# Experts: token numbers kept with an item's rows and stored with y, rows of x loaded two items ahead, routing of tiles 24 to 31 ahead of the queue of side work

## The chip, the cores and the metric

The kernel runs on one core of one Trainium2 chip. The metric is the device time of one launch in microseconds, given as the median of several runs. Beside these stands one profiled execution, from which the trace comes; its time is given apart, since it is not one of the runs of the median.

## The reference

Three layers follow one another, all in float32. Attention has 8 x 8 heads of 576 queries with 64 columns, whose keys and values are averaged over groups of 8 first; its output is read as 4608 tokens x 512 columns. Then each token goes to one of 8 experts, chosen by the cosine of the token with the expert's embedding, and then comes a plain feed-forward layer with h * cos(h) between its two products.

```python
k_p, v_p = mean over groups of 8 of k, v             # 72 keys per head
x = softmax(q @ k_p.T / 8) @ v_p                     # 4608 tokens x 512
logits = (x/|x|) @ (emb/|emb|).T / tau               # 8 experts
expert_idx, gate_w = argmax(logits), softmax(logits)[expert_idx]
for e in range(8):
    h = np.maximum(x[expert_idx == e] @ w1[e], 0.0)  # 512 -> 1024
    out[expert_idx == e] = gate_w * (h @ w2[e])      # 1024 -> 512
h = out @ w_in                                       # 512 -> 2048
return (h * np.cos(h)) @ w_out                       # 2048 -> 512
```

## The kernel before

Every large product is made of three: each operand is split into a rounded high part and the rest (`hi` and `lo`, `xhi` and `xlo`, `ha` and so on), and hi x hi, hi x lo and lo x hi are added up in PSUM. A split is a copy on ScalarE (`w_hi`, line 127, for weights) followed by a subtraction on VectorE or GpSimd (`w_lo`, line 130). The program is written out by hand: the order of the calls is the order of each engine's queue.

**Attention and routing.** `phase_a` goes through 36 tiles of 128 tokens in steps n = -3 to 37 (`step`); a step holds attention for one tile, with products, evacuations and softmax parts of several tiles staggered. After 9, 18, 24, 28, 32, 34 and 36 tiles (`CHUNKS`), `route` gives two lists of short operations for the tiles of the chunk: the gate, the expert and the place `DEST` of each token in its expert's region of the DRAM buffer `xv`. Those lists are put into the queue `side`, from which `pump` takes a few operations at given places of each step. When 32 tiles (`EARLY`) are through, `pick` follows in the same queue: it chooses the expert with the most tokens so far, writes the table `tab0` for the first item, and issues the fetch of its first weights. `scatter(n)` then has GpSimd send a tile's rows to `xv` by an indirect DMA. A row has 514 columns: 512 of x, the gate, and the token's number. After the last step come the scatters left over, the load of the first item's rows, the routing of the last tiles, and the splits of the first weights.

**Expert items.** An item is up to 512 rows of one expert (wide: 8 of them in this run, counting item 0) or 256 (narrow: 5). It has 16 steps k: 8 products of the first layer, `gemm1` (matmuls `ph`, then ReLU and split into `ha`, `hb`), and 8 half products of the second, `gemm2` (matmuls `py`, result in `ys`). Within an item stand, at steps that the tables `FIRST`, `WIDE` and `NARROW` give: the weights' `fetch` and splits for this and the next item, the multiplication of the next item's rows by their gates (`gate`, line 747, ScalarE), and the transposes of these rows (`t_x`: matmuls `ptx` at line 752, then the copy to `xhi` and the subtraction to `xlo`). The rows of the next item come by `x_load` (line 740) at the start of an item, into four buffers `xr`; the item's result goes out at its end by `y_store` into the DRAM buffer `yv`, ordered by item. All loads and stores but the indirect ones are issued by SyncE, in program order; an issue that waits for a buffer holds back those behind it.

In item 0, twelve operations at a time (`LATE`), VectorE works out the tables `tab` of all items between the first-layer products (`tables`); when they are done, zero rows are stored behind each expert's rows, and the loads for item 1 follow (`mid0`). In items 1 to 4 GpSimd sends each tile's token numbers, 4 bytes a token, to their places in the DRAM buffer `pv` (`pos_scatter`, line 797, 36 in all): the feed-forward layer needs them to write its output rows back in token order. `conv_part` converts the feed-forward weights (given as float64) to float32 on VectorE, in 7 short operations for each of 32 pieces, from item 0 on.

**Feed-forward.** In the first narrow item `prepare` loads and splits the first weights and the first 512 columns of input (`f_load`, `f_split`, `x2_load`, `x2_split`). Then nine groups of 512 tokens by 16 slices f follow: `ff1` (matmuls at line 937), `act`, `ff2` (line 961), and the weights are split during the first group, on ScalarE and GpSimd.

## Time and profile before

| | |
|---|---|
| median of three runs | 1595.54 us (1589.47 to 1596.8) |
| the profiled execution | 1583.44 us, of which its span is 1581.70 |
| mean granted TensorE clock | 0.966 of full speed |
| TensorE busy | 1454.1 us, 92% of the span |
| first product of item 0 | 208.05 us after the span's start |
| first product of item 1, of item 5 | 275.45, 506.19 |
| first product of the first narrow item | 647.60 |
| first product of feed-forward | 774.35 |

The span is the profiled execution from its first instruction to its last; what the execution's time has beyond it lies ahead of and behind the program. The lower rows are times on the trace's own clock, from which the length of each stage is read: attention and routing, item 0, items 1 to 4, the other wide items, the narrow items, and feed-forward to the end.

### The profile page before, as it was taken

Reading aid. Unit: us, or ns where it says so; the run is one execution under the profiler, and the core shown is the slowest. Engines: PE = TensorE matmul, PEld = TensorE weight load, DVE = VectorE, ACT = ScalarE, POOL = GpSimd, SP = SyncE. Lnnn points to the kernel's source line nnn. Section 1 sums busy time; section 2 is a strip of 40 time slices with the busy share of each in tenths; the row PEclk is TensorE's granted clock in tenths of the full one; section 3 lists DMA queues with packets and bytes.
Section 4 is the critical chain, followed back from the end, with each engine's and each line's share of the span. In section 5 each row is a group of like instructions: output and inputs, shape, how many; then the busy total and the mean of one; then the engine's idle time right before and its main releaser. Section 6 shows DMA issues by size and latency. Waiting matters only on the chain.

```text
span 1581.7 us, 20523 instructions
## 1 busy us (share of the span) xinstructions
PE 1454.1 (92%) x7480; PEld 1231.9 (78%) x7480; DVE 933.0 (59%) x1623; ACT 609.6 (39%) x1006; POOL 485.1 (31%) x377
## 2 busy tenths in 40 slices
PE   4999667498999999999899999999999999999996
PEld 4898556376777888899787888888888888888885
DVE  5788764365656652344488656565656565565653
ACT  4898533133333444555533222232323222222321
POOL 4578531436553444353444101020201011010200
PEclk9999878789999999999999999999999999999998
DMA  9865437867998655586531101010100000010000
GB/s 264 229 187 151 161 125 231 134 173 192 179 238 216 215 190 170 200 267 214 175 92 56 52 1 54 1 54 1 54 1 27 27 27 28 1 54 1 27 1 27
DMA packets 91877, 177.77 MB, mean 112 GB/s; under 512 B 16236, under 2 KB 35180, under 8 KB 91764
## 3 DMA queue, kind: packets, MB, share of 16 engines
q1 hardware_dynamic: 84688, 157.38, 36.2%
q0 software_dynamic: 6912, 18.94, 3.3%
q8 instruction: 62, 1.02, 0.3%
q14 instruction: 55, 0.42, 0.1%
q10 hardware_dynamic: 160, 0.02, 0.0%
HBM read 135.87 MB, written 40.43 MB: 111 GB/s over the span
## 4 chain that ended last, share of the span: by engine, by line
PE 39%; issue 5%; DVE 4%; ACT 1%; POOL 1%; DVEq 0%; POOLq 0%; ACTq 0%
PE ph L937 20%; PE po L961 20%; DVE xhi L951 2%; DVE ys L947 1%; DVE ys L949 1%; ACT ys L948 1%; DVE co L946 0%; DVE xhi L950 0%; POOL out_dram L972 0%; POOL ha L923 0%; ACT ha L922 0%; ACT ys L945 0%; DVEq L950 0%; POOLq L971 0%; POOLq L972 0%
## 5 line engine op out<-in xcount | busy, mean ns | idle before, releaser
L130 POOL TENSOR_TENSOR lo<-raw,hi 128x1024 fp32r<-128x1024 f32 x82 | 196.6, 2403 | 305.6 <-ACT hi L127 268.7
L945 ACT ACTIVATE ys<-ph,quarter 128x512 f32<-128x512 f32 x144 | 99.0, 688 | 297.1 <-PE ph L937 296.8
L961 PE MATMUL po<-hi,xhi 128*128 128x512 f32 x576 | 178.9, 390 | 0.2
L948 ACT ACTIVATE ys<-ys 128x512 f32<-128x512 f32 x144 | 91.0, 632 | 227.6 <-DVE ys L947 227.6
L951 DVE TENSOR_TENSOR xhi<-ys,xhi 128x512 fp32r<-128x512 f32 x144 | 159.7, 1109 | 5.1
L961 PE MATMUL po<-fh,xhi 128*128 128x512 f32 x504 | 157.1, 392 | 2.8 <-DVE xhi L951 2.2
L949 DVE TENSOR_TENSOR ys<-ys,ph 128x512 f32<-128x512 f32 x144 | 99.1, 688 | 100.6 <-ACT ys L948 100.6
L946 DVE TENSOR_SCALAR co<-ys 128x512 f32<-128x512 f32 x144 | 63.2, 439 | 155.9 <-ACT ys L945 155.9
L762 PE MATMUL ph<-xhi,hi 128*128 128x512 f32 (+1 forms) x416 | 101.2, 366 | 53.7 <-DVE hb L766 36.0
L777 PE MATMUL py<-ha,hi 128*128 128x256 f32 (+1 forms) x576 | 142.6, 340 | 0.1
L961 PEld LDWEIGHTS po<-hi,xhi 128*128 128x128 f32 x576 | 108.2, 188 | 24.8 <-DVE xhi L951 2.5
L762 PEld LDWEIGHTS ph<-xhi,hi 128*128 128x128 f32 x416 | 71.5, 196 | 69.5 <-DVE hb L766 37.6
L127 ACT ACTIVATE hi<-raw 128x1024 fp32r<-128x1024 f32 x108 | 112.1, 1053 | 6.3 <-DMA raw<-in_moe_w_dram 4.9
L961 PEld LDWEIGHTS po<-fh,xhi 128*128 128x128 f32 x504 | 95.0, 188 | 24.4 <-DVE xhi L951 3.8
L961 PE MATMUL po<-lo,xhi 128*128 128x512 f32 x288 | 112.1, 389 | 0.0
L777 PEld LDWEIGHTS py<-ha,hi 128*128 128x128 f32 x576 | 97.9, 193 | 9.7 <-DVE ha L766 0.3
L923 POOL TENSOR_TENSOR hb<-craw,hb 128x1024 fp32r<-128x1024 f32 x10 | 25.1, 2518 | 260.9 <-ACT hb L922 260.9
L947 DVE TENSOR_TENSOR ys<-ys,co 128x512 f32<-128x512 f32 x144 | 99.7, 692 | 4.9
L961 PE MATMUL po<-fl,xhi 128*128 128x512 f32 x252 | 98.6, 391 | 0.0
L762 PE MATMUL ph<-xlo,hi 128*128 128x512 f32 (+1 forms) x416 | 98.4, 360 | 0.0
L762 PE MATMUL ph<-xhi,lo 128*128 128x512 f32 (+1 forms) x416 | 97.0, 356 | 0.0
L777 PE MATMUL py<-ha,lo 128*128 128x256 f32 (+1 forms) x288 | 96.1, 334 | 0.0
(211 smaller groups left out, 2891.4 us busy)
## 6 DMA issues: line engine op xcount, KB each, us to landing
raw<-in_moe_w_dram SPq DMA_DIRECT2D x116, 512.0 KB, 5.5
xr<-xv SPq DMA_DIRECT2D x46, 257.0 KB, 6.8
kraw<-in_k_dram SPq DMA_DIRECT2D x12, 768.0 KB, 9.0
vraw<-in_v_dram SPq DMA_DIRECT2D x8, 1152.0 KB
craw<-yv SPq DMA_DIRECT2D x9, 1024.0 KB, 5.4
q<-in_q_dram SPq DMA_DIRECT2D x8, 1024.0 KB
craw<-in_moe_w_in_dram SPq DMA_DIRECT2D x16, 512.0 KB
craw<-in_moe_w_out_dram SPq DMA_DIRECT2D x16, 512.0 KB, 4.5
```

What stands on the lines that cost most here:

```text
L127: nc.scalar.activation(HI[c], RAW[c], AF.Copy)
L130: eng.tensor_tensor(LO[c], RAW[c], HI[c].bitcast(F32), ALU.subtract)
L762: nc.tensor.matmul(p[:, 0:w], W[kk][:, f * 128:(f + 1) * 128], x[:, kk, 0:w], start=(c == 0), stop=(c == 3 * KC - 1))
L777: nc.tensor.matmul(p[:, 0:w], W[4 + f // 2][:, o:o + 128], h_at(f, m, w), start=(f == 0 and c == 0), stop=(f == FC1 - 1 and c == 2))
L937: nc.tensor.matmul(p, wf(f, s, 0)[:, kk * 128:(kk + 1) * 128], x2[:, m * KC + kk, :], start=(c == 0), stop=(c == 3 * KC - 1))
L945: nc.scalar.activation(u, p, AF.Identity, scale=1.0 / TWO_PI_EXACT, bias=quarter)
L946: nc.vector.tensor_scalar(nr, u, MAGIC, MAGIC, op0=ALU.add, op1=ALU.subtract)
L947: nc.vector.tensor_tensor(u, u, nr, ALU.subtract)
L948: nc.scalar.activation(u, u, AF.Sin, scale=TWO_PI)
L949: nc.vector.tensor_tensor(u, u, p, ALU.mult)
L951: nc.vector.tensor_tensor(gl, u, gh.bitcast(F32), ALU.subtract)
L961: nc.tensor.matmul(O[g][r], a[:, r * 128:(r + 1) * 128], wf(f, s, 1), start=(f == 0 and c == 0), stop=(f == FC2 - 1 and c == 2))
```

## The change

- *Token numbers.* `pos_scatter`, the places `COLI` and their four table steps go. A row's number, which lies in column 513 of `xr`, is transposed by one more TensorE operation per tile in `t_x`, into a PSUM bank `pp`; after an item's last tile ScalarE copies the item's numbers to `pt`, and `pos_store` sends them to `pv`, which is now ordered as `yv` is, by a plain DMA at the start of the item. For the first item the numbers lie in a row of `ys` until then.
- *Rows of x.* `x_load` for the rows of the item after the next one stands at an item's end, ahead of `y_store`, and no longer at the next item's start. The gates of wide items stand after steps 8, 9, 11 and 13, in place of 4 to 7. The weights' fetches move from ahead of steps 8 and 14 to behind 6 and 13.
- *Routing.* The fifth chunk (tiles 28 to 31) is routed at step 33 directly and no longer through `side`, with `pick` in its middle, and its scatters, the load of the first item's rows and the weights' fetch stand in step 34. The `hi` splits of the first weights stand in the last steps; two of the `lo` splits go to GpSimd; the last tiles' second list and their scatters go into the operations of item 0. Item 0's gates stand on VectorE.
- *Zero rows* are stored as soon as the last places are known, ahead of the tables and not behind them.
- *Conversion* in item 0 begins at step 8, in place of 10.
- *Preparation of feed-forward* in the first narrow item: `x2_load` at step 0, in place of 8; `x2_split` at 6 and 7, in place of 13 and 14; three weights are split there on VectorE, in place of one on GpSimd, and more are loaded.

```diff
-    pv = dram.tile([REG + 128, 1], F32, name="pv")
+    pv = dram.tile([1, NT + 512], F32, name="pv")
...
+    def zero_rows():
+
+        for e in range(E):
+            row = nc.sync.value_load(basei[0:1, e:e + 1], min_val=e * REG, max_val=e * REG + NT)
+            d = nc.sync.dma_start(xv[bass.ds(row, 128), :], zeros)
+            apart("xv_rows", d)
+            SENT.append(d)
...
+            if n == EARLY + 2:
+                for f in early[1]:
+                    f()
...
+            if n == EARLY + 2:
+                for f in early[2]:
+                    f()
+                for i in range(EARLY - 4, EARLY):
+                    scatter(i)
+                x_load(tab0, 0, 4)
+                fetch(tab0, 0, 4, 1)
             for c0, c1 in chunks[:-1]:
-                if n == c1 + 1:
+                if n == c1 + 1 == EARLY + 1:
+                    assert c0 == EARLY - 4 and not side and not todo
+                    f1, f2 = route(c0, c1, sm, lambda: misc("pr"))
+                    early.update({1: f1[-1:] + [f2[1], f2[3]] + pick(sm), 2: [f2[0], f2[2]] + f2[4:]})
+                    for f in f1[:-1]:
+                        f()
+                elif n == c1 + 1:
                     f1, f2 = route(c0, c1, sm, lambda: misc("pr"))
                     side.extend(f1[:-2] + [None, f1[-2]] + ([None] if c1 < RL else []) + [f1[-1]] + f2 + [lambda c0=c0, c1=c1: todo.extend(range(c0, c1))])
-                    if c1 == EARLY:
-                        side.extend(pick(sm))
-            if PN <= n <= N:
+            if n >= PN:
                 while todo and todo[0] < EARLY:
                     scatter(todo.pop(0))
             if n < PN:
                 pump(PU, 1)
             else:
                 pump(PF if n <= N else len(side), 2)
+            if n > N - 1:
+                for c in range(2 * (n - N), 2 * (n - N) + 2):
+                    w_hi(c)
...
+        V.tensor_copy(basei, base)
+        V.ops.append(zero_rows)
...
+        def gate(r, first=False):
+            if first:
+                nc.vector.tensor_scalar(xr[r][:, 0:DM], xr[r][:, 0:DM], xr[r][:, DM:DM + 1], None, op0=ALU.mult)
+            else:
+                nc.scalar.activation(xr[r][:, 0:DM], xr[r][:, 0:DM], AF.Copy, scale=xr[r][:, DM:DM + 1])
+
+        PT_ = {}
+
+        def t_x(r, n, b=0, out=1):
             p = bank(b, "ptx")
             for kk in range(KC):
                 nc.tensor.transpose(p[:, kk * 128:(kk + 1) * 128], xr[r][:, kk * 128:(kk + 1) * 128], ident)
             pv_, s = p.rearrange("p (k n) -> p k n", k=KC), slice(r * 128, (r + 1) * 128)
             nc.scalar.activation(XHI[:, :, s], pv_, AF.Copy)
             nc.vector.tensor_tensor(XLO[:, :, s], pv_, XHI[:, :, s].bitcast(F32), ALU.subtract)
+            if r == 0:
+                PT_[0] = bank(6, "pp")
+            nc.tensor.transpose(PT_[0][0:1, s], xr[r][:, DM + 1:XW], ident)
+            if r == n - 1:
+                nc.scalar.activation(pt[out][:, 0:n * 128], PT_[0][0:1, 0:n * 128], AF.Copy)
...
-        def pos_scatter(n):
-            nc.gpsimd.engine_nop()
-            d = nc.gpsimd.indirect_dma_start(
-                out=pv, out_offset=bass.IndirectOffsetOnAxis(ap=COLI[:, n:n + 1], axis=0),
-                in_=GT[:, n, 1:2], in_offset=None,
-            )
-            apart("pos", d)
-            POSD.append(d)
+        def pos_store(i, w, out=1):
+            col = nc.sync.value_load(tab[i:i + 1, 4:5], min_val=0, max_val=NT)
+            nc.sync.dma_start(pv[:, bass.ds(col, w)], pt[out][:, 0:w])
...
-            w1c, w2c, on_dve, gates, txs = when
+            w1c, w2c, on_dve, gates, txs, (at2, at1) = when
             if i:
-                x_load(tab, i + 1, n)
+                pos_store(i, w)
             for k in range(16):
-                if k == 8:
-                    fetch(tab, i + 1, 5, 1)
-                if k == 14 and i:
-                    fetch(tab, i + 2, 5, 0)
                 if k < 8:
                     gemm1(k, w)
-                    if mid:
-                        mid(k)
                 else:
-                    for r in gates.get(k, ()):
-                        gate(r)
                     gemm2(k // 2 - 4, k % 2, w)
                     for r in txs.get(k, ()):
-                        t_x(r)
-                    if mid:
-                        mid(k)
+                        t_x(r, n)
+                if mid:
+                    mid(k)
                 for c in (w2c if k < 8 else w1c).get(k, ()):
                     w_hi(c)
                     w_lo(c, nc.vector if c in on_dve else nc.gpsimd)
+                if k == at2:
+                    fetch(tab, i + 1, 5, 1)
+                if k == at1:
+                    fetch(tab, i + 2, 5, 0)
                 if conv:
                     conv(k)
-                if k < 8:
-                    for r in gates.get(k, ()):
-                        gate(r)
-            if not i:
-                fetch(tab, 2, 5, 0)
+                for r in gates.get(k, ()):
+                    gate(r)
+            x_load(tab, i + 2, n)
...
-        WIDE = {8 + k: (k,) for k in range(4)}, {k: (4 + k,) for k in range(4)}, (), {4 + k: (k,) for k in range(4)}, {9: (0,), 11: (1,), 13: (2,), 15: (3,)}
...
+        WIDE = {8 + k: (k,) for k in range(4)}, {k: (4 + k,) for k in range(4)}, (), {8: (0,), 9: (1,), 11: (2,), 13: (3,)}, {9: (0,), 11: (1,), 13: (2,), 15: (3,)}, (6, 13)
...
-        while todo and todo[0] < EARLY:
-            scatter(todo.pop(0))
-        x_load(tab0, 0, 4)
-        fetch(tab0, 0, 4, 1)
-        f1, f2 = route(NTILE - CHUNKS[-1], NTILE, const, lambda: bank(6, "pr"))
         while todo:
             scatter(todo.pop(0))
-        for f in f1:
+        f1, f2 = route(NTILE - CHUNKS[-1], NTILE, const, lambda: bank(7, "pr"))
+        for f in f1[:-1]:
             f()
-        for c in range(4):
-            w_hi(c)
-            w_lo(c, nc.vector)
-        for f in f2:
-            f()
-        for i in range(NTILE - CHUNKS[-1], NTILE):
-            scatter(i)
-        zeros = second_part()
-        late = tables(co[0], craw[0][:, 0, :])
+        pt.append(ys[0:1, 3, :])
         for r in range(4):
-            gate(r)
+            gate(r, True)
         for r in range(4):
-            t_x(r, (0, 3, 4, 5)[r])
...
-        def mid0(n):
-            if n < 8:
+            t_x(r, 4, (0, 3, 4, 5)[r], 0)
+            w_lo(r, nc.vector if r < 2 else nc.gpsimd)
+        f1[-1]()
+        second_part()
+        late = f2 + [lambda: [scatter(i) for i in range(NTILE - CHUNKS[-1], NTILE)]] + tables(ys[:, 0, :])
+
+        def mid0(k):
+            if k < 8:
                 for f in late[:LATE]:
                     f()
                 del late[:LATE]
-                if not late and zeros is not None and not once:
+                if not late and not once:
                     once.append(1)
-                    zero_rows(zeros)
+                    pos_store(0, 512, 0)
                     x_load(tab, 1, 4)
                     fetch(tab, 1, 5, 0)
-                    conv_load(0)
-                    conv_load(1)
+                    for j in range(2):
+                        conv_load(j)
 
         once = []
-        item(0, 512, conv_part(0, 10, 16), mid0, FIRST)
+        item(0, 512, conv_part(0, 8, 16), mid0, FIRST)
         assert once
         for i in range(1, NW0):
-            item(i, 512, conv_part(i, 0, 16), lambda k, i=i: pos_scatter((i - 1) * 9 + k) if k < 9 else None, WIDE)
...
         def prepare(k):
             if k == 0:
                 f_load(0)
-            if k == 8:
                 x2_load(0)
-            if k == 10:
-                f_split(0)
-            if k in (13, 14):
-                x2_split(0, k - 13)
+            if k == 5:
+                f_split(0, nc.vector)
+            if k in (6, 7):
+                x2_split(0, k - 6)
+            if k == 7:
+                for f in range(1, 4):
+                    f_load(f)
+            if k in (13, 15):
+                f_split(1 + k // 15, nc.vector)
             if k == 15:
-                for f in range(1, 4):
+                for f in (4, 5):
                     f_load(f)
...
-        f_split(1)
         seq = [(g, f) for g in range(NG) for f in range(FC2)]
         NS = len(seq)
         for n in range(NS + 2):
-            if n + 2 < FC2:
-                f_split(n + 2)
-                if 4 <= n + 4 < FC2:
-                    f_load(n + 4)
+            if n + 3 < FC2:
+                f_split(n + 3)
+                if n + 6 < FC2:
+                    f_load(n + 6)
```

Three places show how this moves instructions. The first is SyncE's queue at the end of an item; L785 and L811 are the store of an item's result, L740 and L234 the loads of rows into `xr`, L815 is the store of token numbers. Before, at the end of item 0 and the start of item 1:

```order
L784 TENSOR_LOAD tab
L784 ISA x2
L785 REGISTER_ALU
L785 DMA yv<-ys 512x1x512
L739 TENSOR_LOAD tab
L739 ISA x2
L740 ISA
L740 DMA xr_102<-xv 128x514
L739 TENSOR_LOAD tab
L739 ISA x2
L740 ISA
L740 DMA xr_103<-xv 128x514
```

and now, from the last of the four row loads on:

```order
L233 TENSOR_LOAD tab
L233 ISA x2
L234 ISA
L234 DMA xr_105<-xv 128x514
L810 TENSOR_LOAD tab
L810 ISA x2
L811 REGISTER_ALU
L811 DMA yv<-ys 512x1x512
L814 TENSOR_LOAD tab
L814 ISA x2
L815 REGISTER_ALU
L815 DMA pv<-pt 1x512
```

All four row loads now stand ahead of the store; the numbers' store of the item that begins follows it.

The second place is ScalarE in the first narrow item, around its last first-layer products; `ha` is the ReLU of a product, L127 the high part of a weight, L747 and L766 the gate, L781 and L807 the result, L754 and L775 the copy of transposed rows, L910 and L916 the split of a feed-forward weight, L926 that of the feed-forward input. Before:

```order
L765 ACTIVATE ha<-ph 128x256 x2
L127 ACTIVATE hi_2525<-raw_114 128x1024
L765 ACTIVATE ha<-ph 128x256
L747 ACTIVATE xr_102<-xr_102 128x512
L765 ACTIVATE ha<-ph 128x256
L747 ACTIVATE xr_103<-xr_103 128x512
L127 ACTIVATE hi_98<-raw_107 128x1024
L781 ACTIVATE ys<-py 128x256
L754 ACTIVATE xhi<-ptx 128x4x128
L127 ACTIVATE hi_99<-raw_108 128x1024
L910 ACTIVATE fh_2634<-ys 128x1024
```

and now:

```order
L791 ACTIVATE ha<-ph 128x256 x2
L916 ACTIVATE fh_2657<-ys 128x1024
L127 ACTIVATE hi_2583<-raw_114 128x1024
L791 ACTIVATE ha<-ph 128x256
L926 ACTIVATE hb<-craw 128x1024
L791 ACTIVATE ha<-ph 128x256
L926 ACTIVATE hb<-craw 128x1024
L766 ACTIVATE xr_102<-xr_102 128x512
L127 ACTIVATE hi_98<-raw_107 128x1024
L807 ACTIVATE ys<-py 128x256
```

The feed-forward weight stood behind the item's first result and now stands ahead of its last two `ha`; the splits of the input, which stood at the item's end, follow these two.

The third place is VectorE where the first expert is chosen, in attention's last steps; L430 to L432 and L448 to L450 belong to a tile's attention output, L383 and L401 are the maximum of the last tiles' scores, L203 to L213 are `pick`. Before:

```order
L430 TENSOR_TENSOR lp<-pav,rd 128x64
L431 TENSOR_TENSOR x<-pav,rd 128x512
L432 TENSOR_REDUCE LG<-lp 128x8
L203 TENSOR_TENSOR pc<-base,ebase 128x8
L204 TENSOR_REDUCE pm<-pc 128x1
L205 TENSOR_SCALAR pt<-pc,pm 128x8
L206 TENSOR_TENSOR pt<-pt,idx_73 128x8
L207 TENSOR_REDUCE pk_2280<-pt 128x1
L208 TENSOR_SCALAR first_e<-idx_73,pk_2280 128x8
L209 TENSOR_SCALAR pk_2280<-pk_2280 128x1
L210 TENSOR_SCALAR tab_93<-pk_2280 128x1
L426 TENSOR_SCALAR rd<-pav 128x8
```

and now, with the same maximum that before stands some way ahead of these rows:

```order
L401 TENSOR_REDUCE mx<-psc 128x8
L185 TENSOR_TENSOR rt_2310<-pr,base 128x32
L187 TENSOR_TENSOR base<-base,pr 128x8
L203 TENSOR_TENSOR pc<-base,ebase 128x8
L204 TENSOR_REDUCE pm<-pc 128x1
L205 TENSOR_SCALAR pt<-pc,pm 128x8
L206 TENSOR_TENSOR pt<-pt,idx_73 128x8
L207 TENSOR_REDUCE pk_2314<-pt 128x1
L208 TENSOR_SCALAR first_e<-idx_73,pk_2314 128x8
L209 TENSOR_SCALAR pk_2314<-pk_2314 128x1
L210 TENSOR_SCALAR tab_92<-pk_2314 128x1
L211 TENSOR_SCALAR tab_92<-pk_2314 128x1
```

The two operations of `route` on which the choice rests (L185, L187) and the choice itself now follow that maximum directly; the rest of `route` comes behind them.

## Rows read from the trace of the kernel before

**Rows 1.** The page, part 1: busy time of TensorE, its share, its matmuls.
```profile
PE 1454.1 (92%) x7480; PEld 1231.9 (78%) x7480; DVE 933.0 (59%) x1623; ACT 609.6 (39%) x1006; POOL 485.1 (31%) x377
```

**Rows 2.** Timeline of TensorE: start, length in us; last, the wait before and who ended it.
```profile
203.65 3.67 PE L752 MATMUL ptx<-ident,xr 128*128 128x128 f32 x16 [9.87 <-ACT xr L747]
208.05 2.05 PE L762 MATMUL ph<-xhi,hi 128*128 128x512 f32 x4 [0.73 <-issue]
227.77 2.07 PE L762 MATMUL ph<-xhi,hi 128*128 128x512 f32 x4 [6.58 <-DVE ha L766]
265.37 1.11 PE L752 MATMUL ptx<-ident,xr 128*128 128x128 f32 x4 [7.30 <-DVE xlo L755]
275.45 1.44 PE L762 MATMUL ph<-xhi,hi 128*128 128x512 f32 x4 [0.74 <-ACT xhi L754]
318.83 1.65 PE L762 MATMUL ph<-xhi,hi 128*128 128x512 f32 x3 [23.77 <-DVE hb L766]
506.19 1.19 PE L762 MATMUL ph<-xhi,hi 128*128 128x512 f32 x4 [0.80 <-ACT xhi L754]
552.68 1.19 PE L762 MATMUL ph<-xhi,hi 128*128 128x512 f32 x4 [0.80 <-ACT xhi L754]
647.60 0.73 PE L762 MATMUL ph<-xhi,hi 128*128 128x256 f32 x4 [2.75 <-ACTq L1023]
774.35 1.16 PE L937 MATMUL ph<-hb,fh 128*128 128x512 f32 x4 [2.75 <-PEq L1046]
787.66 0.51 PE L961 MATMUL po<-fh,xhi 128*128 128x512 f32 x1 [2.19 <-DVE xhi L951]
```

**Rows 3.** The loads of token rows (L740): who waited for them; time to landing.
```profile
  ACT xr L747: 51.2, 6
DMA to landing us min/median/max: 2.6/6.8/26.9
```

**Rows 4.** Timeline of SyncE's queue in the second item.
```profile
289.82 6.60 SPq L740 DMA_DIRECT2D xr<-xv  x4
```

**Rows 5.** DMA from 288 to 318 us: all packets, then the queue of GpSimd's DMAs.
```profile
DMA packets 2330, 4.97 MB, mean 166 GB/s; under 512 B 436, under 2 KB 568, under 8 KB 2330
q0 software_dynamic: 256, 0.00, 2.1%
```

**Rows 6.** DMA from 510 to 525 us, when no token number is scattered.
```profile
DMA packets 1983, 3.61 MB, mean 241 GB/s; under 512 B 144, under 2 KB 573, under 8 KB 1981
```

**Rows 7.** Groups by line, GpSimd: the scatters of token numbers, busy us and mean ns.
```profile
L797 POOL DMA_INDIRECT pv<-GT,COLI x36 | 35.0, 973 | 8.6 <-issue 8.6
```

**Rows 8.** Timeline of TensorE: four transposes of one tile of token rows.
```profile
254.73 0.60 PE L752 MATMUL ptx<-ident,xr 128*128 128x128 f32 x4
```

**Rows 9.** Timeline of VectorE and SyncE's queue at the end of attention.
```profile
176.34 0.76 DVE L383 TENSOR_REDUCE mx<-psc 128x8 f32<-128x576 f32 x1
184.10 0.16 DVE L203 TENSOR_TENSOR pc<-base,ebase 128x8 f32<-128x8 f32 x1
197.62 2.60 SPq L740 DMA_DIRECT2D xr<-xv  x3
```

**Rows 10.** Timeline of GpSimd and VectorE while the first item's weights are split.
```profile
217.41 9.34 POOL L130 TENSOR_TENSOR lo<-raw,hi 128x1024 fp32r<-128x1024 f32 x4 [3.71 <-ACT hi L127]
217.52 2.38 DVE L634 TENSOR_TENSOR co<-co 128x64 f32<-128x64 f32 x1
```

**Rows 11.** Timeline of VectorE where the first conversion of feed-forward weights begins.
```profile
259.65 0.69 DVE L860 TENSOR_SCALAR ca<-craw 128x512 uint32<-128x512 uint32 x1 [17.00 <-DMA craw<-in_moe_w_in_dram]
264.64 0.68 DVE L755 TENSOR_TENSOR xlo<-ptx,xhi 128x512 fp32r<-128x512 f32 x1
```

**Rows 12.** Timeline of SyncE's queue in the first narrow item.
```profile
645.14 0.60 SPq L785 DMA_DIRECT2D yv<-ys  x1
660.88 0.66 SPq L914 DMA_DIRECT2D craw<-yv  x1
```

**Rows 13.** The loads of feed-forward input (L914): time to landing.
```profile
DMA to landing us min/median/max: 5.4/5.4/5.5
```

71 lines of the change are left out of this document (26 added, 45 removed).

## The prediction

> **What bounds the kernel now.** I read the page first: TensorE is busy for 92% of the span [rows 1], so the kernel can lose time only where TensorE waits or has its clock lowered. The second view is TensorE's timeline, of which I kept the matmuls that had waited and the first matmul of some items [rows 2]. The reader is to see that two wide items in a row without a wait are 552.68 - 506.19 = 46.49 us apart, and that the four items from 275.45 to 506.19 take 230.74 us where 4 x 46.49 = 185.96 would do: 44.8 us are lost in items 1 to 4. The longest single wait there is 23.77 us. It names VectorE's `hb`, which waits in turn for ScalarE, and ScalarE stands at the gating of the next item's rows: the third view, the loads of `xr`, gives 51.2 us of such waiting in six places, and a slowest landing of 26.9 us against a fastest of 2.6 [rows 3]. Fourth, the DMA: while that slow load (issued from 289.82 on [rows 4]) is under way, 4.97 MB move at 166 GB/s, and the queue with the 4-byte scatters of token numbers takes only 2.1% itself [rows 5]; four items later, when no number is scattered, much the same mix (a y store, four row loads, a conversion) moves at 241 GB/s [rows 6] and nobody waits. Ahead of item 1 lie a wait of 9.87 us for the first item's rows, and waits of 6.58 and 7.30 us inside item 0 [rows 2].
>
> **The change part by part.** The sum is made against the profiled execution's own 1583.44 us (span 1581.70 and 1.74 around it). That lies 12.1 us under the median of the three runs, 1595.54; I apply the same difference to the median.
>
> *Items 1 to 4.* The 36 scatters on GpSimd, 973 ns each [rows 7], go. The load of rows stands at almost the same place in SyncE's queue as before, but ahead of the y store instead of behind it, and the gate moves from after product 4 to after step 8, so four steps of 46.49 / 16 = 2.9 us, 11.6 us, are added to the time that a load may take. Items 5 to 7, where nothing was scattered, had no wait even with the early gate. I take the whole 44.8 us: -44.8. The other bound is -30, if the second item's load is late once more (below). GpSimd's freed 35 us are worth nothing by themselves, since its splits were waited for nowhere in these items.
>
> *Token numbers through TensorE.* Each tile of rows gets one more transpose, one column wide. No row shows such a column; the nearest is four transposes of full width in 0.60 us [rows 8], so 0.15 each as the upper price and 0 as the lower. There are 8 x 4 + 5 x 2 = 42 tiles; the last one of each of the 13 items falls into the wait for `xhi` that stands ahead of the next item anyway (0.74 to 0.80 us [rows 2]), so 29 x 0.15 = 4.4: +4. ScalarE's copy of the numbers and the 2 KB store are one each per item and lie beside the first products of the next item, which leave both idle; without that cover 13 copies at 0.69 (a step of 512 columns) would cost 9.
>
> *Routing of tiles 28 to 31.* The choice of the first expert now begins behind the maximum at 176.34 (0.76 long), not at 184.10 [rows 9]: 7.0 us earlier, and with it the fetch of the first weights on SyncE. The rows come later than that: their load, at 197.62 now, waits for the last scatters of x, whose four descriptors GpSimd still writes one after the other, and the work that used to lie behind it (the splits of LO, the last tiles' routing) is moved off the path. Attention itself pays for some 20 short VectorE operations put ahead of a tile's own. Between 0 and -7 I take -5 for the start of item 0 at 208.05.
>
> *Inside item 0.* The tables run beside GpSimd's four splits of the second weights (217.41, 9.34 us), and a table step that takes two operands from SBUF stands 2.38 us there [rows 10]; that is the 6.58 us wait. The splits and the tables both stay, the tail of routing (11 short steps) now stands ahead of the tables, so the wait moves one product on and keeps its size. The zero rows leave the middle of the queue, so row, weight and conversion loads are issued earlier; but conversion begins two steps earlier in the program too, and ten of its steps, not seven (7 took 264.64 - 259.65 = 5.0 us [rows 11]), now stand on VectorE ahead of the first `xlo`. What is won on arrival is mostly spent in that line: -2, with bounds of -13.9 (both waits gone) and +5.
>
> *Feed-forward preparation in the first narrow item.* The load of the feed-forward input is now the third DMA of that item, where before it stood behind the second weights and was issued at 660.88 [rows 12]; it lands 5.4 us after issue [rows 13]. ScalarE has its copies of that data, and of the first feed-forward weights, ahead of the `ha` of products 6 and 7. Those fall due about 647.60 + 7 x 1.45 = 657.8 (half of 2.9 a step). The load must wait for the y store of 645.14 to land; with 5.4 for that megabyte too and some 3.5 for the end of the branch and the two DMAs ahead, I estimate its issue at 654 and its arrival at 659.5, so ScalarE, and behind it VectorE's `lo` and TensorE's second layer, are some 2 us late. SyncE then waits for GpSimd to empty the buffer before it may fetch the next weights, which have an item's length to spare. +3; bounds 0, and 660.88 + 5.4 - 657.8 = +8.5 if the load goes out no sooner than now.
>
> *Start of feed-forward.* Three instead of one split weight are ready at 774.35. The 2.19 us wait at 787.66 [rows 2] goes, and one GpSimd split fewer lies beside the loop: -2.5, between 0 and -3.
>
> On the shared access of VectorE and GpSimd the row comes first: 2.38 us for a small operation beside a running split [rows 10]. The Trainium skill says of this (SBUF, State Buffer, section Who interferes with whom) that a VectorE instruction with two SBUF inputs is blocked until the GpSimd instruction that reads SBUF has ended; the trace agrees. It speaks against this change, which gives VectorE three splits of that kind in an item where GpSimd splits too; the third rival below is its price.
>
> Sum: -44.8 + 4 - 5 - 2 + 3 - 2.5 = -47.3. The profiled execution would come to 1536.1, the median to 1548.2 us.
>
> **The rivals.** First, *both waits in item 0 go as well*: the conversion data are there before step 8 and the tables slip past the splits. For it: the conversion's wait is a wait for a DMA [rows 11], which is issued earlier now. Against it: the splits on GpSimd are unchanged. 11.9 us more than forecast, 1536.3.
>
> Second, *the rows still land late in the second item*. The slow window had its time in the hardware queue, not in the 2.1% of the scatters [rows 5]; if y store, weight fetch and rows slow each other, the scatters were bystanders. Issued 14.4 us into the item as now (289.82 - 275.45) and landing after 26.9, the rows come at 41.3; the gate stands at 8 x 2.9 = 23.2 and its use one step on: 15 us of wait, 1563.2. Against it: rows 6, and the y store now follows. The Trainium skill (DMA: Bandwidth & Descriptors, Specifications) asks for transfers of at least 512 B and has smaller ones read, modify and write; it does not say that other queues suffer. If only the scatters' own share of the 30 us window is saved, 0.6 us, this rival holds; no run here shows yet which it is.
>
> Third, *VectorE blocked by GpSimd in the narrow item*: three splits of 9.34 / 4 = 2.34 us each stand behind one on GpSimd and hold back the `lo` steps in line behind them: 7.0 us, 1555.2. For it: row 10's block. Against it: GpSimd has pauses between its splits.
>
> Fourth, on the other side, *the one-column transposes are dear*: TensorE is the bound, and nothing hides 29 to 42 of them. The gain without them is 51.3 us, so they decide from 51.3 / 42 = 1.22 us each on; to be slower by over 0.5% (8 us, about what a measurement of this kernel can tell from no change) they would need 1.4. Nearest row: 0.15. At 1.5 the time is 1595.5 - 51.3 + 63 = 1607.
>
> Last, *the change does not do what it says*: the row load hardly moves in the queue, and if the gate's new place only shifts the wait from ScalarE's gate to the transposes behind it, some 5 us remain: 1590.
>
> **How the numbers follow.** Forecast 0.58, all waits in item 0 gone 0.14, rows still late 0.12, blocked splits 0.10, no effect 0.03, dear transposes 0.03. The time is the forecast's, 1548. Its own range is 1540 to 1557 (its terms' smaller bounds). The range for 8 in 10 runs from 1531, a little under the first rival, to 1566, a little over the second. Faster by over 0.5%: 0.94; within it: 0.03; slower: 0.03.
>
> **What would show it.** In the new profile: no wait of ScalarE at the gate for `xr` over 1 us in items 1 to 4, and item starts 46.9 us apart there; a DMA rate near rows 6 at the start of item 1; first product of item 0 near 203; a wait of 5 to 8 us at product 5 of item 0 and another ahead of its second transpose; one wait of 2 to 3 us in the first narrow item at the second half of its first output; no 2 us wait at the second step of feed-forward. The prediction is wrong if the starts of items 1 to 4 stay over 50 us apart, or if a wait that stood nowhere before appears once per item.

## The result and the profile after

The changed kernel takes 1540.09 us (median of four runs, 1536.69 to 1541.52); the kernel before, run with it, 1596.17 (1589.47 to 1600.46). The ratio is 0.9649, with a 95% interval of 0.9612 to 0.9687: faster by 3.5%. The forecast was 1548.2. The profiled execution took 1541.52 us, 41.9 less than the one before; the forecast's sum was 47.3.

The page, part 1 (busy time) and part 3 (queues) of the kernel after:

```profile
PE 1456.0 (95%) x7526; PEld 1234.7 (80%) x7526; DVE 935.2 (61%) x1624; ACT 612.7 (40%) x1016; POOL 448.2 (29%) x340
...
q1 hardware_dynamic: 85290, 158.45, 32.5%
q0 software_dynamic: 5760, 18.92, 3.3%
```

TensorE does as much as before [rows 1], plus 46 one-column transposes, in 42 us less. Its timeline, to be read against [rows 2]:

```profile
206.07 1.09 PE L773 MATMUL ptx<-ident,xr 128*128 128x128 f32 x4 [9.88 <-DVE xr L764]
210.58 1.17 PE L788 MATMUL ph<-xhi,hi 128*128 128x512 f32 x4 [0.54 <-issue]
231.07 2.07 PE L788 MATMUL ph<-xhi,hi 128*128 128x512 f32 x4 [8.05 <-DVE ha L792]
266.02 1.11 PE L773 MATMUL ptx<-ident,xr 128*128 128x128 f32 x4 [4.34 <-DVE xlo L776]
276.22 1.21 PE L788 MATMUL ph<-xhi,hi 128*128 128x512 f32 x4 [0.69 <-ACT xhi L775]
323.67 1.21 PE L788 MATMUL ph<-xhi,hi 128*128 128x512 f32 x4 [0.69 <-ACT xhi L775]
370.54 1.21 PE L788 MATMUL ph<-xhi,hi 128*128 128x512 f32 x4 [0.69 <-ACT xhi L775]
464.29 1.21 PE L788 MATMUL ph<-xhi,hi 128*128 128x512 f32 x4 [0.69 <-ACT xhi L775]
607.21 0.74 PE L788 MATMUL ph<-xhi,hi 128*128 128x256 f32 x4 [3.00 <-ACTq L1019]
737.19 2.08 PE L941 MATMUL ph<-hb,fh 128*128 128x512 f32 x4 [4.50 <-ACTq L1046]
749.75 0.50 PE L965 MATMUL po<-fh,xhi 128*128 128x512 f32 x1 [1.80 <-DVE xhi L955]
```

The four items from 276.22 to 464.29 take 188.07 us where they took 230.74, and no wait in them is over 0.7 us. Against that the first product of item 0 comes later (210.58, before 208.05), and the wait inside item 0 is longer (8.05, before 6.58). Time to landing of the row loads in these items, from 276 to 520 us, before (line L740) and after (line L234); [rows 3] has the whole run:

```profile
DMA to landing us min/median/max: 9.4/19.4/26.9
...
DMA to landing us min/median/max: 3.0/3.4/4.9
```

TensorE's clock is a part of the gain. Items 1 to 4 and item 0, before and then after: length of the stretch, TensorE's busy time, its granted clock, the DMA's share, GB/s:

```profile
275.45:506.19 230.74, 191.66 (x832) 0.91 0.86 186
208.05:275.45 67.40, 52.77 (x209) 0.84 0.50 169
...
276.22:464.29 188.07, 185.01 (x849) 1.00 0.68 224
210.58:276.22 65.64, 51.55 (x213) 0.87 0.54 183
```

In the four items before, TensorE waited for 39.0 us, and for 41.0 us, in and behind the long waits, the granted clock stood at 0.5 (1.2 GHz in place of 2.4). After, it waits for 3.1 us and the clock stays at 1.0. So 36 of the 42.7 us are waits. Of the 41.0 us, 16 fell on work and not on waiting, which at half speed is a loss of some 8 us (an estimate); 36 + 8, less 2.1 that the items grew by (188.07 against 4 x 46.49), make about the 42.7.

The same difference by stages, in us, from the two traces (first products of item 0, item 1, item 5, the first narrow item and feed-forward, the end of the last matmul, and the span's end):

| stage | before | after | moved | forecast |
|---|---|---|---|---|
| attention and routing | 208.05 | 210.58 | +2.5 | -5 |
| item 0 | 67.40 | 65.64 | -1.8 | -2 |
| items 1 to 4 | 230.74 | 188.07 | -42.7 | -44.8, and the transposes |
| items 5 to 7 | 141.41 | 142.92 | +1.5 | the transposes |
| narrow items | 126.75 | 129.98 | +3.2 | +3, and the transposes |
| feed-forward to the last matmul | 793.45 | 791.59 | -1.9 | -2.5 |
| last matmul to the end | 13.90 | 11.02 | -2.9 | 0 |

(The transposes were +4 over all items.) The sum is -41.9.

### The profile page after: what moved, and what is told of

The parts are those of the page before. It is cut to its first block, busy times and chain, and to the rows that moved or that the text cites. A ratio compares the mean times of both kernels' runs of the same rounds, so it can differ in the third digit from the quotient of the medians.

```text
span 1539.8 us, 20664 instructions
## 1 busy us (share of the span) xinstructions
PE 1456.0 (95%) x7526; PEld 1234.7 (80%) x7526; DVE 935.2 (61%) x1624; ACT 612.7 (40%) x1016; POOL 448.2 (29%) x340
## 4 chain that ended last, share of the span: by engine, by line
PE 45%; issue 5%; DVE 1%; POOL 0%; ACT 0%; POOLq 0%; DVEq 0%; ACTq 0%
PE ph L941 23%; PE po L965 22%; DVE xhi L955 0%; POOL out_dram L976 0%; DVE ys L951 0%; DVE ys L953 0%; DVE co L950 0%; ACT ys L952 0%; DVE xhi L954 0%; ACT ys L949 0%; POOLq L975 0%; DVEq L954 0%; DVEq L955 0%; POOLq L976 0%; POOLq L1135 0%
## 5 line engine op out<-in xcount | busy, mean ns | idle before, releaser
L130 POOL TENSOR_TENSOR lo<-raw,hi 128x1024 fp32r<-128x1024 f32 x84 | 202.0, 2410 | 303.2 <-ACT hi L127 257.8
L955 DVE TENSOR_TENSOR xhi<-ys,xhi 128x512 fp32r<-128x512 f32 x144 | 155.5, 1080 | 5.1
L788 PE MATMUL ph<-xhi,hi 128*128 128x512 f32 (+1 forms) x416 | 97.7, 358 | 17.5 <-DVE ha L792 8.8
L127 ACT ACTIVATE hi<-raw 128x1024 fp32r<-128x1024 f32 x108 | 112.8, 1053 | 2.3 <-SPq L1019 2.0
```

The costliest lines, as they stand in the source:

```text
L127: nc.scalar.activation(HI[c], RAW[c], AF.Copy)
L130: eng.tensor_tensor(LO[c], RAW[c], HI[c].bitcast(F32), ALU.subtract)
L788: nc.tensor.matmul(p[:, 0:w], W[kk][:, f * 128:(f + 1) * 128], x[:, kk, 0:w], start=(c == 0), stop=(c == 3 * KC - 1))
L955: nc.vector.tensor_tensor(gl, u, gh.bitcast(F32), ALU.subtract)
```

## The experiments

My theory was that the 4-byte scatters hold up the loads of rows, and that their end is worth the 44.8 us. The main rival: load and gate stood in a bad place, and the scatters were bystanders. The runs came in three groups of four, each group on one chip, and each but the last is a single execution; the kernel before took 1592.77 us beside the first, 1589.57 beside the second, and 1584.48 (median of 11) beside the third.

**The kernel before, once more.** No edit.

> The kernel before, profiled a second time, since its first profile (1583.44 us) lay 12 us under its median. Theory: the row loads that are late beside the scatters vary from run to run, so the difference lies in items 1 to 4 (230.7 us in the first profile), and attention, item 0, the narrow items and feed-forward repeat within 2 us. Rival: the difference lies in TensorE's granted clock (0.966 in the first profile) and is spread over all stages.

1588.86 us, span 1587.1. Items 1 to 4 took 235.30 us (before: 230.74): 4.6 of the 5.4 us between the two spans. The rival falls, since the clock is the same (0.967 against 0.966). The other stages repeat within 1 us, as expected. The late rows of the kernel before differ from run to run, and its first profile was a good one; that is a part of why the medians differ by 56 us where the two profiles differ by 42.

**The scatters added again**, and alone.

```diff
-            item(i, 512, conv_part(i, 0, 16), None, WIDE)
+            item(i, 512, conv_part(i, 0, 16), lambda k, i=i: pos_scatter((i - 1) * 9 + k) if k < 9 else None, WIDE)
```

> The changed kernel with the 36 scatters of token numbers added again in items 1 to 4, into a spare buffer that nothing reads; load of rows and gates stay at their new places. Theory (the scatters hold up the loads of rows): the loads land 15 to 27 us after issue again; the second item's rows, issued 4.7 us into the item, land about 31.6 us into it, and their first transpose is due at 29.3, so one wait of 2 to 5 us there, and the four items take 190 to 195 us instead of 188.1. Rival (the old place of load and gates was the cause, the scatters were bystanders): loads land within 10 us, no wait, 188 us.

1576.38 us; the four items took 219.98, not 190 to 195. The cause is as expected and the size is not, for the delay came out elsewhere. This trace has no landing times for the loads of rows, so the 15 to 27 us can't be read; ScalarE waited for no row at its gate. Timelines of SyncE's queue, VectorE and TensorE in the second item:

```profile
287.49 0.37 SPq L865 DMA_DIRECT2D craw<-in_moe_w_out_dram  x1
...
308.09 0.69 DVE L875 TENSOR_SCALAR ca<-craw 128x512 uint32<-128x512 uint32 x1 [10.59 <-DMA craw<-in_moe_w_out_dram]
308.70 0.68 DVE L793 SCALAR_TENSOR_TENSOR hb<-ph,hb 128x512 fp32r<-128x512 f32 x1
...
309.43 0.80 PE L804 MATMUL py<-hb,hi 128*128 128x512 f32 x1 [6.18 <-DVE hb L793]
```

It is a conversion load now: issued at 287.49, there at 308. VectorE stands at it, and behind it in VectorE's line stands the `hb` that TensorE needs. The DMA from 276 to 464 us says why. The changed kernel:

```profile
DMA packets 20961, 42.07 MB, mean 224 GB/s; under 512 B 1506, under 2 KB 6626, under 8 KB 20947
q1 hardware_dynamic: 20947, 41.90, 68.2%
```

And this one:

```profile
DMA packets 18378, 34.97 MB, mean 186 GB/s; under 512 B 2181, under 2 KB 6346, under 8 KB 18365
q1 hardware_dynamic: 17447, 34.80, 95.0%
q0 software_dynamic: 918, 0.02, 0.4%
```

The scatters' own queue takes 0.4%, but the other queue's packets now take 95.0 / 34.80 = 2.73% per MB where they took 68.2 / 41.90 = 1.63%: 1.7 times as long. So the scatters slow the other queue as a whole, not the rows alone. The Trainium skill (DMA: Bandwidth & Descriptors, Specifications) has transfers under 512 B read, modify and write; no run here shows that step by itself.

**The old place of load and gates, no scatters.**

```diff
             if i:
+                x_load(tab, i + 1, n)
                 pos_store(i, w)
...
-            x_load(tab, i + 2, n)
             y_store(i, w)
```

(and the gates of `WIDE` at steps 4 to 7, of `NARROW` at 6 and 7)

> The changed kernel with the load of rows at the next item's start and the gates of wide and narrow items at their old steps; no scatters. Theory (the scatters hold up the loads of rows): the loads land in under 10 us, no wait of ScalarE over 2 us at the gate in items 1 to 4, and the four items take 187 to 191 us. Rival (the place of load and gates was the cause): loads of 15 to 27 us, the four items take over 215 us.

1542.88 us. TensorE's timeline shows its wide items as far apart as in the changed kernel:

```profile
322.83 1.21 PE L788 MATMUL ph<-xhi,hi 128*128 128x512 f32 x4 [0.69 <-ACT xhi L775]
369.70 1.21 PE L788 MATMUL ph<-xhi,hi 128*128 128x512 f32 x4 [0.69 <-ACT xhi L775]
```

And the loads of rows landed as fast:

```profile
DMA to landing us min/median/max: 3.0/3.7/5.0
```

The rival falls. With the scatters gone, the new place is worth nothing in wide items: neither place loses time there. With the scatters, both do: the new place 31.9 us (219.98 against 188.07), the old one 42.7. So the scatters are the cause; how much the place adds to what they cost is not shown, since the kernel before differs in other points too. In the narrow items the old place costs 3.4 us (133.40 against 129.98).

**Each one-column transpose twice.**

```diff
             nc.tensor.transpose(PT_[0][0:1, s], xr[r][:, DM + 1:XW], ident)
+            nc.tensor.transpose(PT_[0][0:1, s], xr[r][:, DM + 1:XW], ident)
```

> The changed kernel with each one-column transpose issued twice. Items now start 46.87 us apart, 0.38 more than before. Theory: that is the price of four one-column transposes, 0.095 us each, so the distance becomes 47.25 and the whole run 3 to 4 us longer (42 x 0.095 = 4.0, of which 29 are in the open). Rival: the 0.38 come from something else in the item (the later gates, the moved fetches), and the distance stays within 0.1 of 46.87.

```profile
369.13 1.21 PE L789 MATMUL ph<-xhi,hi 128*128 128x512 f32 x4 [0.58 <-ACT xhi L775]
416.28 1.21 PE L789 MATMUL ph<-xhi,hi 128*128 128x512 f32 x4 [0.58 <-ACT xhi L775]
```

1542.40 us, 2.3 over the changed kernel's median where 3 to 4 were expected; a single run can't tell these apart. Wide items are 47.15 us apart: 0.28 for four, 0.07 each. Of the 0.38 that an item grew, 0.28 are the transposes; the rest has another cause, so theory and rival each hold in part. Two in a narrow item cost 0.23.

**Attention's end: scatters spread, and a slower pace of side work.** The change also quickens the pace of the side work from step 29 on (`PB` from 31 to 29, `PN` from 35 to 29), which its list above does not have. In the changed kernel's profile VectorE and ScalarE read TensorE's results late several times, twice of them while GpSimd issues ten scatters in a row; the maximum of the last tiles (L401) comes at 182.54, where it came at 176.34 [rows 9]:

```profile
168.33 0.81 ACT L424 ACTIVATE atT<-pta 96x768 f32<-96x768 f32 x1 [2.50 <-remote]
172.77 0.17 DVE L444 TENSOR_SCALAR rd<-pav 128x8 f32<-128x8 f32 x1 [3.67 <-PE pq L377]
182.54 0.75 DVE L401 TENSOR_REDUCE mx<-psc 128x8 f32<-128x576 f32 x1
```

```diff
-            if n >= PN:
+            if n >= EARLY + 1:
                 while todo and todo[0] < EARLY:
                     scatter(todo.pop(0))
```

> The changed kernel with the scatters of x spread again: from step 29 to 32 two per step, and all that are due only from step 33 on (before: all that are due from step 29 on, which the trace shows as ten on GpSimd in one row from 159 to 173 us). Attention's last steps take longer in the changed kernel: the maximum of tile 31 stands 1 us earlier than before and that of tile 33 5 to 6 us later. Theory A (the row of scatters holds the other engines up): tile 33's maximum at 168 to 170, first product of item 0 at 205 to 208. Theory B (the routing steps that are pumped earlier stand ahead of a tile's own on VectorE): no change, 173 and 210 to 212.

1534.39 us: tile 33's maximum at 167.98, item 0 at 206.87, as theory A has it. But two kernels of the same group with the changed kernel's attention (the splits behind the tables, the rows of narrow items, both below) have that maximum at 171.68 and 171.05 and item 0 at 208.44 and 207.59. Beside them the edit is worth 3 to 4 us at the maximum and only 0.7 to 1.6 at item 0. The other edit:

```diff
-PI, PT, PB = 1, 3, 29
+PI, PT, PB = 1, 1, 29
```

> The changed kernel with one side operation instead of three at each of the three places inside a step from step 29 on; the six at the step's end stay, so that nine instead of fifteen per step are put between a tile's own. Theory B (the pumped routing steps hold attention up): tile 33's maximum 2 to 4 us earlier than its 173 to 174, first product of item 0 at 207 to 209. Theory A (the row of scatters does): no change, within 1 us.

1540.84 us, with the maximum at 175.84 and item 0 at 212.83: later, not earlier. That is neither theory's sign, and it can't settle theory B, since VectorE now stands for a routing step that GpSimd has behind six scatters in its queue:

```profile
169.21 0.17 DVE L184 TENSOR_SCALAR rn<-rn 128x4 f32<-128x4 f32 x1 [5.64 <-POOL rn L167]
```

Nor did theory A last. Two kernels of the third group have attention exactly as the changed kernel has it, with the same row of scatters, and no such delay:

```profile
168.17 0.75 DVE L401 TENSOR_REDUCE mx<-psc 128x8 f32<-128x576 f32 x1
170.58 0.17 DVE L444 TENSOR_SCALAR rd<-pav 128x8 f32<-128x8 f32 x1 [0.87 <-PE pav L432]
```

(VectorE of the kernel with the conversion loads first, below.) Over the eight traces with this code, item 0 begins between 201.66 and 212.11. The delay goes with the group: between 150 and 190 us ScalarE stands idle for over 2 us ahead of an `atT` copy in every trace of the first two groups, and in both of the kernel before, and in none of the third group's four. Since each group had one chip, chip and chance can't be told apart here. What delays these readers is open.

**The early routing undone**, in the third group: old place of route, choice, fetches and first splits, old pace.

```diff
-PI, PT, PB = 1, 3, 29
+PI, PT, PB = 1, 3, 31
...
-PU, PN = 1, 29
+PU, PN = 1, 35
```

(and the three blocks of `step` with `early` and `w_hi` back as before)

> The changed kernel with the routing of tiles 28 to 31, the choice of the first expert, its fetches and the first weights' high parts back at their old places, and the old pace of side work and scatters. Theory (the early routing gains 3 us behind the last maximum and loses more than that ahead of it): the maximum of tile 33 at 167 to 169, 31 us from the last maximum to item 0's first product (28.4 in the runs of the changed kernel), first product at 207 to 209. Rival (the early routing is a gain, and the start of item 0 has another cause): first product at 213 or later.

1532.99 us. From tile 29's maximum to item 0's first product it took 204.18 - 149.82 = 54.4 us; the two kernels with early routing of this group took 53.1 and 52.8. Behind the last maximum early routing gains 3.2 (31.2 against 28.0 and 27.8), ahead of it it loses 1.8. So it is worth 1.4 us where attention is not delayed: the theory is right on the 3 us behind the maximum and wrong on the larger loss ahead of it, and the rival's 213 did not come.

**The splits behind the tables.** VectorE and GpSimd in item 0 of the changed kernel:

```profile
220.38 9.83 DVE L666 TENSOR_TENSOR ys<-ys 128x8 f32<-128x8 f32 x1
230.34 0.68 DVE L792 SCALAR_TENSOR_TENSOR ha<-ph,ha 128x512 fp32r<-128x512 f32 x1
...
220.90 9.29 POOL L130 TENSOR_TENSOR lo<-raw,hi 128x1024 fp32r<-128x1024 f32 x4
```

A table step on 128 x 8 numbers stands until all four splits are through; before, a step stood for one split at a time [rows 10]. The `ha` behind it is TensorE's 8.05 us.

```diff
-        FIRST = {11 + k: (k,) for k in range(4)}, {1: (4, 5, 6, 7)}, (1, 3), {9: (0,), 10: (1,), 11: (2,), 12: (3,)}, {k: (k - 12,) for k in range(12, 16)}, (8, 15)
+        FIRST = {11 + k: (k,) for k in range(4)}, {1: (4, 5), 6: (6,), 7: (7,)}, (1, 3, 4, 5), {9: (0,), 10: (1,), 11: (2,), 12: (3,)}, {k: (k - 12,) for k in range(12, 16)}, (8, 15)
```

> The changed kernel with item 0's splits of the second weights taken apart: two of the four on VectorE behind product 1, the other two on GpSimd behind products 6 and 7, when the tables are through. Theory (a table step with two operands in SBUF stands as long as GpSimd splits; one stood 9.83 us beside four splits, and TensorE waited 8.05 us at product 5): no table step over 2.5 us, the wait at product 5 under 2 us, item 0 takes 58 to 61 us instead of 65.6, the run is 5 to 7 us shorter. Rival (the tables' own length sets the wait): it stays over 5 us.

1530.52 us. The wait at the fifth product is gone, and item 0 takes 264.31 - 208.44 = 55.9 us, less than the 58 to 61 expected; the clock (below) gives the rest:

```profile
208.44 1.16 PE L788 MATMUL ph<-xhi,hi 128*128 128x512 f32 x4 [0.54 <-issue]
254.05 1.12 PE L773 MATMUL ptx<-ident,xr 128*128 128x128 f32 x4 [4.70 <-DVE xlo L776]
264.31 0.98 PE L788 MATMUL ph<-xhi,hi 128*128 128x512 f32 x3 [0.69 <-ACT xhi L775]
```

The other wait stays (4.70, changed kernel 4.34).

**The conversion loads first.**

```diff
         def mid0(k):
+            if k == 0:
+                for j in range(2):
+                    conv_load(j)
...
                     fetch(tab, 1, 5, 0)
-                    for j in range(2):
-                        conv_load(j)
```

> The changed kernel with the first two conversion loads issued at item 0's first step, not behind the loads for item 1. VectorE stands 12 us at the first conversion step for its data, and ten of its steps stand ahead of the first rest of transposed rows, for which TensorE waits 4.3 us. Theory (it is the data's arrival and VectorE's line): the wait at the second tile's transposes is under 1 us, item 0 takes 59 to 62 us. Rival (rows or weights of item 1 come as late): it stays over 3 us, named by another engine.

1528.86 us; the wait for transposed rows is gone, the 8.04 at the fifth product stays, item 0 takes 58.99:

```profile
203.82 1.16 PE L788 MATMUL ph<-xhi,hi 128*128 128x512 f32 x4 [0.54 <-issue]
224.21 2.08 PE L788 MATMUL ph<-xhi,hi 128*128 128x512 f32 x4 [8.04 <-DVE ha L792]
262.81 1.21 PE L788 MATMUL ph<-xhi,hi 128*128 128x512 f32 x4 [0.69 <-ACT xhi L775]
```

**Rows of narrow items loaded later.**

```diff
+                if n == 2 and k == 1 and i > NROW:
+                    x_load(tab, i + 1, n)
...
-            x_load(tab, i + 2, n)
+            if n == 4:
+                x_load(tab, i + 2, n)
             y_store(i, w)
```

> The changed kernel with the load of rows in narrow items moved from the item's end to step 1 of the next one. The wait ahead of feed-forward grew from 2.75 to 4.50 us, and SyncE's queue shows two row loads that nobody needs ahead of the last store. Theory (every engine leaves the branch only when SyncE has issued the last store, which stands behind these loads): the wait ahead of feed-forward is 2.6 to 3.2 us, the run is 1 to 2 us shorter, and narrow items stay 24.6 us apart. Rival (the wait comes from the weights' fetch or the branch itself): it stays over 4 us.

1538.28 us. The last store went out at 731.28, 4 us ahead of feed-forward, and the wait was still 4.35: the theory falls.

```profile
731.28 0.59 SPq L811 DMA_DIRECT2D yv<-ys  x1
...
735.12 1.66 PE L944 MATMUL ph<-hb,fh 128*128 128x512 f32 x4 [4.35 <-ACTq L1049]
```

**The old preparation of feed-forward.**

```diff
             if k == 0:
                 f_load(0)
+            if k == 8:
                 x2_load(0)
-            if k == 5:
-                f_split(0, nc.vector)
-            if k in (6, 7):
-                x2_split(0, k - 6)
+            if k == 10:
+                f_split(0)
+            if k in (13, 14):
+                x2_split(0, k - 13)
```

(and no other early split, and the old order in the feed-forward loop)

> The changed kernel with the old preparation of feed-forward: input loaded at step 8, one weight split on GpSimd, and the old order of splits in the feed-forward loop. Theory (three splits ready at the start save one GpSimd split and a wait in the loop; in the first narrow item the early preparation costs about 1 us): the first narrow item 1 us shorter, 25.3 to 25.8, the stretch from feed-forward's first product to the end 806 to 807.5 us instead of 802.6. Rival (the 4.7 us come from the order of loads or from chance): under 804.

1535.91 us. From feed-forward's first product to the end 805.76 us, against 802.71 in the kernel with the conversion loads first: 3.05 for the new preparation. The narrow items took 130.45 us, against 130.80, so it costs 0.4 there at most by this pair. The 805.76 lie just under the theory's 806 to 807.5, but the first narrow item took 26.27, not 25.3 to 25.8: that part of the theory fails. The wait ahead of feed-forward was 4.70, so that does not come from the preparation either.

**Three edits together**: scatters spread, splits behind the tables, conversion loads first, timed in five rounds.

> Three edits of single places together in the changed kernel: the scatters of x spread over attention's last steps, item 0's second splits apart from the tables, and the first two conversion loads at item 0's first step. The first two gave about 3.5 us at the start of item 0 and 8 to 10 us in item 0 when tried alone; the third should free the 4.3 us that TensorE waits in item 0 for transposed rows. Theory (the three waits lie one behind the other and are gained in full): 1521 to 1527 us. Rival (each wait hides another, mostly the arrival of rows and weights in item 0): over 1530.

1521.72 us (median of six), ratio to the kernel before 0.9603, interval 0.9581 to 0.9625, which still touches the changed kernel's own (0.9612 to 0.9687). Item 0 takes 49.59 us and has no wait over 0.9:

```profile
204.35 1.16 PE L788 MATMUL ph<-xhi,hi 128*128 128x512 f32 x4 [0.54 <-issue]
253.94 1.20 PE L788 MATMUL ph<-xhi,hi 128*128 128x512 f32 x4 [0.58 <-ACT xhi L775]
```

It lies 7 us under the kernel with one of the three edits on the same chip, and both waits of item 0 were gained in full. The spread scatters brought nothing here: item 0 begins at 204.35, and at 203.82 and 201.66 in the two kernels of this group that have early routing without them. Item 0 gained 16.05 us, more than its two waits of 8.05 and 4.34. In the changed kernel the granted clock stood at 0.5 (1.2 GHz) from 226.2 to 236.4 and from 263.8 to 270.6, falling in each wait and rising behind it, and the four matmuls behind the first wait took 2.07 us, where the item's first four take 1.17. Here it is 1.00 throughout item 0:

```profile
204.35:253.94 49.59, 47.12 (x213) 1.00 0.67 229
```

## Why the prediction was right, and where not

*Items 1 to 4* (-44.8): right. 42.7 were gained; of the other 2.1, 1.1 are the transposes there, and 1.0 has no cause shown. The two runs on scatters and place show the cause. But the reasons I gave were too narrow in three ways: without scatters the later place gives nothing, some of the loss was TensorE's lowered clock, and with the scatters the late rows would not have been the only loss. My bound of -30 and the second rival both hung on the rows alone.

*Transposes* (+4): right in sum, partly by luck: 0.07 each in a wide item and 0.11 in a narrow one, in place of 0.15, but for all of them and not 29, with 0.10 more a wide item from something else.

*Routing of tiles 28 to 31* (-5): wrong, the step that failed. I took the maximum at 176.34 as fixed and moved the choice up behind it. The choice does follow it directly, but the maximum itself came at 182.54, so the choice began at 183.71, 0.4 us earlier and not 7.0. The rows, on which the start of item 0 hangs, come later still: their load was issued 1.8 us later than before [rows 9], and VectorE's gates waited for it.

```profile
183.71 0.17 DVE L203 TENSOR_TENSOR pc<-base,ebase 128x8 f32<-128x8 f32 x1
199.42 4.14 SPq L234 DMA_DIRECT2D xr<-xv  x4
```

From the last maximum to item 0 the change gained 3.7 us in this pair of profiles (28.04 in place of 31.71). Where nothing delays attention, the same edit gains 3.2 us behind the maximum and loses 1.8 ahead of it: -1.4. The 2 that I left off for the side work were about right; the 7.0 was not, since behind the maximum the gain is 3 to 4. The delay on top of it, seen in six of eight traces with this code, was not in the sum and its cause is open.

*Inside item 0* (-2): -1.8 in this profile, right in size by luck. The nine traces with this item 0 have 62.4 to 65.6 us, the kernel before 67.4 and 67.9: the longer ones had the clock at 0.5 for 17 us, the shorter ones for 10 to 11. The wait stayed at the fifth product and did not move on and keep its size, as I had said it would; it grew to 8.05. The first rival (both waits gone) is what the two edits of single places make of it, 49.6 us instead of 65.6, but not this change. The row of 9.83 us is one VectorE step that stood for four GpSimd splits in a row. The Trainium skill (SBUF — State Buffer, Who interferes with whom) has a VectorE instruction with two SBUF inputs contend with a GpSimd instruction that reads SBUF, for ports that one of them holds alone; the trace agrees as far as one split goes. In the kernel before, the splits followed each other without a gap as well, and four table steps stood in turn, each (up to 2.38 us) until one split ended. Why the step here, which began 0.5 us ahead of the first split, stood through all four is open.

*Preparation in the first narrow item* (+3): the stage grew by 3.2 us, for another reason. The input was there in time, and the wait that I had named did not show, so the size is luck. 1.1 are transposes (0.22 in each of five items), 1.75 the longer wait ahead of feed-forward (4.50, before 2.75), which I had not seen. It was 2.75 and 2.44 in the two traces of the kernel before and 3.5 to 5.0 in all twelve with the change, also with the row loads moved or the old preparation; it is open.

*Start of feed-forward* (-2.5): right, 3.05 by the run that undoes it, though only 1.9 between the two profiles, and the wait at the second step that I wrote off is still there (1.80). Up to the end of the last matmul the eleven kernels with the new preparation take 790.1 to 792.7 us, the one without 794.8, the kernel before 793.5 and 793.1. The third rival, blocked splits on VectorE, cost nothing: the three splits took 1.23, 1.97 and 1.23 us, and TensorE waits nowhere in that item.

*The end*, which I had not counted: from the last scatter of the output to the span's end 7.8 us, before 10.7. It goes with the scatters of token numbers: the kernel that has them again takes 10.7.

The sum missed the two profiles' difference by 5.4 us: 7.5 too much on routing, less the end's 2.9, and under 1 on each of the rest. The median came out 8.1 under the forecast all the same, since I had added to it the 12.1 us by which the first profile of before lay under its median. The second profile shows part of that to be the late rows' own chance, which the change takes away: the changed kernel's profile lies 1.4 above its median. So two errors of opposite sign stand in the forecast of the median. The range of 1531 to 1566 holds the result, and no rival's own sign (a wait that takes the old one's place, dear transposes) showed.

## What to carry to other kernels

Judge a stream of tiny writes not by its own share of a queue but by what the other queue's packets take per MB while it runs. An engine that reads its operations in order turns any late transfer into a wait of whatever stands behind: taking one victim out of the way (a later gate) moves much of the loss to the next (31.9 of 42.7 us here). A wait can cost more than its own length, where the granted clock falls in it and the work behind it runs at half speed. And a term that rests on "the same moment as before" for work whose own surroundings the change also touches needs bounds on both sides of zero.

## What the runs showed of the hardware

36 scatters of 128 four-byte values, 0.4% of the DMA time, made each MB of the other queue take 1.7 times as long (2.73% against 1.63% of 188 us). With them in the program its end, from the last output scatter to the span's end, took 10.7 us in three traces, without them 7.8 in eleven. In all ten traces in which item 0's four GpSimd splits stand behind a table step, that VectorE step of 128 x 8 numbers stood 9.81 to 9.83 us, until the last split was through; beside four such splits in the kernel before, no step stood over 2.38. In item 0 of the changed kernel the granted clock was at 0.5 for 17 us around two waits of 8.05 and 4.34 us; with both waits gone it was at 1.0, and the item 16.05 us shorter.
